# Transposes, copies and differences of an expert's rows in separate steps, and token tables in every second step

## The chip, the core and the metric

The kernel runs on one core of one Trainium2 chip. The time is the device time of one execution in microseconds (us), the median of three runs. A core has a matrix engine (TensorE, PE in the rows, PEld for its weight loads), VectorE (DVE), ScalarE (ACT), GpSimd (POOL) and SyncE (SP), which issues most DMAs. Each engine has its own list of instructions and works through it; semaphores hold an instruction until what it reads is there.

## The reference

Windowed attention, then a mixture of experts, then a gated feed-forward layer. The change lies in the middle part:

```python
def _moe_ref(x, w_gate, w_output_gate, w1, w2):     # x: 2304 x 512, 8 experts, w1: 8 x 512 x 1024, w2: 8 x 1024 x 512
    logits = x @ w_gate
    e_idx = np.argmax(logits, axis=1)
    ...
    for e in range(E):
        mask = e_idx == e
        h = np.maximum(x[mask] @ w1[e], 0.0)
        ye = h @ w2[e]
        out[mask] = gate_w[mask, None] * eom[mask, e, None] * ye
    return out
```

## The kernel before

The attention stage ends with every token's row scattered into the DRAM tensor xs, sorted by expert. The experts are ranked by size; rank p gets room for caps[p] rows: 384, 384, 352, 336, 304, 272, 256, 256. "Expert 3" below is rank 3.

The loop of the expert stage treats experts 0 to 6, each in 16 steps. Steps 0 to 7 are the first layer: step m computes one block of 128 hidden features on TensorE (L1423, tile oh), ScalarE writes its relu hh (L1431), VectorE the remainder hl (L1437). Every number is held as a high part and a low part, which is why each product takes three passes: high rows with high weights, low rows, then low weights. Steps 8 to 15 are the second layer: step kk multiplies block kk of hh and hl into four output tiles oy (L1447). The last expert and the dense layer follow from a table of steps written out by hand, in which the last expert's first layer is L1217.

Behind the matmuls of every step, behind_step does work for later. It takes up to two items of weights that SP has loaded: for an expert's weight ScalarE copies the high part (L461, tile w) and VectorE, or GpSimd for every third, subtracts to get the low part (L463). A 64-bit weight of the dense layer takes two ScalarE operations (L405, L406) and two merges on VectorE (L412, L417). As each item frees its staging tile (there are seven), w_load issues the next load on SP. After that, behind_step draws once from the generator tokens, that is token_order followed by overflow_tables (L890 to L1014). These are small VectorE operations that work out which token each sorted row belongs to, three groups of six comparisons (L941, tile tbl), each followed by six small matmuls on TensorE (L947, tile oid_ps) and a sum (L952, L954), and at the end the tables of overflow blocks, which two DMAs of ScalarE's queue (L1009, L1014) write to DRAM. The generator has 40 pieces, drawn in the steps of experts 0 and 1 and of expert 2's first layer.

In the first four steps of an expert's second layer, emit_xT prepares the rows of the next expert: VectorE transposes a quarter of the features (L1067, tile t, two buffers), ScalarE copies it rounded (L1070, xh), and VectorE forms the difference (L1071, xl). In step 12 (kk = 4) load_x loads the rows of the expert after that into xr, which has one buffer, by four DMAs on SP.

For expert 0 the transposes are made on TensorE instead (L1075 to L1077); that part stays.

The order on every engine in this stage is the order of the code (a manual schedule). The functions that the change touches:

Of the kernel before, what the change touches and what calls it, by code (L numbers as in the profile page):

```python
# [7 lines left out]
F32 = mybir.dt.float32  # L8
# [5 lines left out]
AF = mybir.ActivationFunctionType  # L14
ALU = mybir.AluOpType
# [131 lines left out]
def attn_moe_glu_kernel(ctx, tc, q, k, v, w_gate, w_ogate, w1, w2, w2_gate, w2_val, w2_out, out, caps=CAPS):  # L147
    nc = tc.nc
    B, H, S, D = q.shape
    NT, DM = out.shape  # L150
    E = w_gate.shape[1]
# [8 lines left out]
    KD = DM // 128  # L160
    KF = FF // 128
    KF2 = FF2 // 128
    cap = max(caps)
    CB = -(-cap // 128)
    CP = CB * 128
# [48 lines left out]
    with ExitStack():  # L214
# [811 lines left out]
        def pair_tile(pool, tag, w):  # L1026
            return [pool.tile([128, w], F32R, tag=tag + x, name=tag + x) for x in "hl"]

        def grid(t, n, w):
            return t[:, 0:n * w].rearrange("p (k c) -> p k c", k=n)  # L1030
# [23 lines left out]
        def emit_xT(p, kks=range(KD)):  # L1054
            if p >= E:
                return
            n = caps[p]
            cb = -(-n // 128)
            r = xr[p]
            if p not in xe:  # L1060
                xe[p] = [grid(t, KD, n) for t in pair_tile(xe_p, "x", KD * cap)]
            xh, xl = xe[p]
            for kk in kks:
                if p:
                    nb = -(-n // 32)
                    t = s_p.tile([128, CP], F32, tag="sc", name="t")
                    nc.vector.transpose(  # L1067
                        out=t[:, 0:nb * 32].rearrange("p (b i) -> p b i", i=32), in_=r.rearrange("p b (i k) -> p k b i", k=KD)[:, kk]
                    )
                    nc.scalar.activation(out=xh[:, kk, :], in_=t[:, 0:n], func=AF.Copy)  # L1070
                    TT(out=xl[:, kk, :], in0=t[:, 0:n], in1=xh[:, kk, :], op=ALU.subtract)  # L1071
                    continue
                t = ps_m.tile([128, CP], F32, tag="m", name="tx")
                for c in range(cb):
                    nc.tensor.transpose(t[:, c * 128:c * 128 + 128], features(r[:, c, 0:DM], kk), ident)  # L1075
                nc.scalar.activation(out=xh[:, kk, :], in_=t[:, 0:n], func=AF.Copy)
                TT(out=xl[:, kk, :], in0=t[:, 0:n], in1=xh[:, kk, :], op=ALU.subtract)  # L1077

        yr, x2 = {}, {}

        xraw = [None, None]

        PASSES = ((0, 0), (0, 1), (1, 0))
        HW = KF * cap
# [19 lines left out]
        def behind_step(i0=0):  # L1104
            for i in range(i0, len(plan[step_no[0]])):
                behind_item(i)
            step_no[0] += 1
            if step_no[0] <= E * STEPS:
                next(tokens, None)

        UW = 2 * WU
# [296 lines left out]
        with tc.manual_schedule(engines=ALL_ORDERED):  # L1408
# [5 lines left out]
            for p in range(E - 1):  # L1414
# [29 lines left out]
                for kk in range(KF):  # L1444
                    for d in range(KD):
                        for i, (a, b) in enumerate(PASSES):
                            nc.tensor.matmul(  # L1447
                                out=o[d][:, 0:n],
                                lhsT=wt["w2", p, 0, kk][:, a, d * 128:d * 128 + 128],
                                rhs=(hh, hl)[b][:, kk, :],  # L1450
                                start=(kk == 0 and i == 0),
                                stop=(kk == KF - 1 and i == 2),
                            )
                    if kk % 2:
                        freed[0] += 1
                    if p + 1 < E:
                        if kk < KD:
                            emit_xT(p + 1, (kk,))
                    if kk == KD:
                        if p + 2 < E:  # L1460
                            load_x(p + 2)
                    behind_step()
# [142 lines left out]
```

## Time and profile before

| | |
|---|---|
| median of 3 runs | 828.47 us (828.15 to 829.36) |
| the profiled execution | 831.0 us, of which the span of the trace is 829.3 us |
| TensorE busy in the span | 786.4 us (95%) |
| VectorE busy | 669.2 us (81%) |
| ScalarE busy | 505.2 us (61%) |
| GpSimd busy | 165.0 us (20%) |

The profile shows one execution. Busy time is what an engine spent in instructions; a matmul's end is modelled, so that a busy TensorE is not one at its peak. The granted clock (PEclk) is a share of TensorE's full speed. A wait is the idle time of an engine ahead of an instruction, with the instruction whose end released it; several causes are put down to the last.

### The profile page before, as it was taken

The page shows a single profiled execution, that of the slowest core. Times are in us where ns is not written, and L with a number is a line of the kernel's source. Part 1 is how long each engine was busy: PE and PEld are TensorE (multiplying, and loading weights), DVE is VectorE, ACT ScalarE, POOL GpSimd, SP SyncE. Part 2 cuts the span into 40 slices and gives each one's busy share as a digit, 9 for nine tenths or more (in the row PEclk, how much of TensorE's full clock was granted, in tenths as well). Part 3 has the DMA queues.
Part 4 walks back from the last instruction along what each step waited for, and adds up shares of the span by engine and source line. Part 5 has one row for each costly group of instructions (what it writes and reads, how often), then busy time and mean ns, then how long its engine had stood idle before and what let it go on. Part 6 is the DMA issues. An engine that isn't in the chain of part 4 may idle for free.

```text
span 829.3 us, 17503 instructions
## 1 busy us (share of the span) xinstructions
PE 786.4 (95%) x6031; PEld 727.7 (88%) x6031; DVE 669.2 (81%) x1771; ACT 505.2 (61%) x1355; POOL 165.0 (20%) x249
## 2 busy tenths in 40 slices
PE   8999998979998998798999999999999999999995
PEld 6887784979998998797999999999999999999994
DVE  7899786685887886878999999999877799777642
ACT  6999871445546675666876766765555465554432
POOL 5477775031112122221000000030000003000003
PEclk9999999999998999989999999999999999999998
DMA  9999924867586796797125221131311103111112
GB/s 186 242 222 313 283 92 141 262 204 232 163 250 199 244 281 204 248 279 245 64 65 177 102 102 64 52 115 65 126 51 52 52 26 128 51 52 51 28 50 79
DMA packets 120815, 121.16 MB, mean 146 GB/s; under 512 B 63634, under 2 KB 79634, under 8 KB 120722
## 3 DMA queue, kind: packets, MB, share of 16 engines
q1 hardware_dynamic: 113184, 106.31, 43.6%
q0 software_dynamic: 2880, 9.48, 3.0%
q10 hardware_dynamic: 4658, 4.20, 1.5%
q8 instruction: 49, 0.80, 0.4%
q14 instruction: 44, 0.36, 0.2%
HBM read 89.23 MB, written 30.73 MB: 145 GB/s over the span
## 4 chain that ended last, share of the span: by engine, by line
PE 34%; issue 33%; DVE 11%; DMA 9%; ACT 8%; POOL 2%; SPq 1%; ACTq 0%; DVEq 0%; POOLq 0%
PE pa L1297 6%; PE oo L1320 6%; PE pb L1297 5%; PE oh L1423 4%; DMA rawd<-in_moe_w_gate_dram 3%; PE o L615 3%; ACT w L461 2%; PE s L524 2%; DVE t L1067 2%; POOL out_dram L1335 2%; DVE w L463 2%; PE oh L1217 2%; PE tp L592 1%; DVE rawd L412 1%; DMA raw<-in_moe_w_dram 1%
## 5 line engine op out<-in xcount | busy, mean ns | idle before, releaser
L1320 PE MATMUL oo<-xh,hw 128*128 128x512 f32 x432 | 133.3, 390 | 0.0
L1297 PE MATMUL pa<-w 128*128 128x384 f32 x630 | 127.9, 338 | 0.8 <-ACT wtmp L1158 0.6
L1297 PEld LDWEIGHTS pa<-w 128*128 128x128 f32 x630 | 112.2, 188 | 9.4 <-ACT wtmp L1158 1.3
L1447 PE MATMUL oy<-hh,w 128*128 128x384 f32 (+5 forms) x448 | 103.1, 316 | 0.4 <-DVE hl L1437 0.4
L1335 POOL DMA_INDIRECT out_dram<-ob,oid x18 | 20.5, 1137 | 417.0 <-ACT ob L1158 292.0
L1297 PE MATMUL pb<-w 128*128 128x384 f32 x468 | 94.5, 336 | 0.0
L1423 PE MATMUL oh<-xh,w 128*128 128x384 f32 (+5 forms) x448 | 82.6, 323 | 10.9 <-ACT xh L1070 9.2
L463 POOL TENSOR_TENSOR w<-raw,w 128x512 fp32r<-128x512 f32 x37 | 49.5, 1339 | 193.3 <-ACT w L461 134.9
L1320 PEld LDWEIGHTS oo<-xh,hw 128*128 128x128 f32 x432 | 79.6, 187 | 6.4
L1158 ACT ACTIVATE w<-w 128x256 fp32r<-128x256 f32 (+2 forms) x168 | 76.2, 462 | 14.3 <-DVE w L1185 10.4
L1320 PE MATMUL oo<-xl,hw 128*128 128x512 f32 x216 | 84.4, 391 | 0.0
L1423 PEld LDWEIGHTS oh<-xh,w 128*128 128x128 f32 x448 | 72.9, 197 | 12.6 <-ACT xh L1070 10.5
L1297 PEld LDWEIGHTS pb<-w 128*128 128x128 f32 x468 | 82.7, 188 | 0.4 <-DVE wtmp L1373 0.3
L1447 PEld LDWEIGHTS oy<-hh,w 128*128 128x128 f32 x448 | 77.1, 190 | 1.0 <-DVE hl L1437 0.9
L1158 ACT ACTIVATE wtmp<-pa 128x384 f32<-128x384 f32 x72 | 35.5, 493 | 65.1 <-PE pa L1297 64.8
L461 ACT ACTIVATE w<-raw 128x512 fp32r<-128x512 f32 x112 | 67.7, 623 | 6.3 <-ACT y L1092 5.0
L1447 PE MATMUL oy<-hl,w 128*128 128x384 f32 (+5 forms) x224 | 70.5, 315 | 0.0
L1158 ACT ACTIVATE w<-wraw 128x256 fp32r<-128x256 f32 x108 | 44.6, 415 | 41.4 <-PE pa L1297 25.6
L1373 DVE TENSOR_TENSOR wtmp<-pb,wtmp 128x384 f32<-128x384 f32 x72 | 40.1, 557 | 32.4 <-ACT wtmp L1158 26.3
L1370 DVE TENSOR_TENSOR wtmp<-wtmp 128x384 f32<-128x384 f32 x108 | 58.6, 555 | 6.1 <-ACT wtmp L1376 5.5
L463 DVE TENSOR_TENSOR w<-raw,w 128x512 fp32r<-128x512 f32 x75 | 57.2, 773 | 5.8 <-ACT w L461 4.6
L578 ACT ACTIVATE p<-p,mn 128x128 f32<-128x128 f32 x144 | 56.4, 408 | 0.4 <-DVE mn L557 0.3
(259 smaller groups left out, 1679.9 us busy)
## 6 DMA issues: line engine op xcount, KB each, us to landing
raw<-in_moe_w_dram SPq DMA_DIRECT2D x128, 256.0 KB, 4.3
xs<-zrow SPq DMA_DIRECT2D x8, 774.0 KB, 7.4
rawd<-in_moe_w_gate_dram SPq DMA_DIRECT2D x24, 256.0 KB, 5.0
rawd<-in_moe_w_val_dram SPq DMA_DIRECT2D x24, 256.0 KB, 2.9
rawd<-in_moe_w_out_dram SPq DMA_DIRECT2D x24, 256.0 KB, 3.4
xh<-wo_s SPq DMA_DIRECT2D x24, 256.0 KB, 2.6
xl<-wo_s SPq DMA_DIRECT2D x24, 256.0 KB, 2.9
w<-ys SPq DMA_DIRECT2D x6, 768.0 KB, 6.3
```

The costliest lines, as they stand in the source:

```text
L461: nc.scalar.activation(out=s[:, 0, :], in_=t, func=AF.Copy)
L463: (nc.gpsimd if n_rows[0] % 3 == 0 else nc.vector).tensor_tensor(out=s[:, 1, :], in0=t, in1=s[:, 0, :], op=ALU.subtract)
L578: last_exp[0] = nc.scalar.activation(out=pr[:, c, :], in_=pr[:, c, :], func=AF.Exp, bias=mn[:, c:c + 1], scale=-1.0, accum_out=sums[j][:, ...
L615: nc.tensor.matmul(out=o[64 * a:64 * a + 64, 2 * hf + pp, :], lhsT=raw["vr", j - 1 + i][:, 4 * hf + 2 * pp + a, :], rhs=pm[:, i, 2 * pp + ...
L1158: nc.scalar.activation(out=out, in_=in_, func=AF.Copy)
L1297: nc.tensor.matmul(out=bank_of(j), lhsT=w[:, a, k, :], rhs=x_at(j, b, k), start=(n == 0 and j in (0, 1, 5)), stop=(n == 5), skip_group_che ...
L1320: nc.tensor.matmul(out=o_w[c], lhsT=h_at(s, t)[b][:, b0 * 128:b0 * 128 + 128], rhs=wo_at(s, a), start=(kk == 0 and i == 0), stop=(kk == KF ...
L1335: r = nc.gpsimd.indirect_dma_start(out=out[:, :], out_offset=bass.IndirectOffsetOnAxis(ap=oid[:, 2 * WB * pr + c, :], axis=0), in_=ob, in_ ...
L1370: TT(out=out, in0=a, in1=b, op=ALU.mult)
L1373: TT(out=temp(i), in0=bank_of(j), in1=temp(k), op=ALU.add)
L1423: nc.tensor.matmul(out=o[:, 0:n], lhsT=wt["w1", p, m // 4, kk][:, a, (m % 4) * 128:(m % 4) * 128 + 128], rhs=(xh, xl)[b][:, kk, :], start= ...
L1447: nc.tensor.matmul(out=o[d][:, 0:n], lhsT=wt["w2", p, 0, kk][:, a, d * 128:d * 128 + 128], rhs=(hh, hl)[b][:, kk, :], start=(kk == 0 and i ...
```

## The change

emit_xT keeps only the part for expert 0. A new function turn_step(p + 1, kk), called in every step of the second layer, issues at step i the difference of quarter i - 2, then the transpose of quarter i, then the copy of quarter i - 1. So a quarter's three operations stand in three successive steps, and the group ends in step 5 of the second layer (kk = 5) instead of step 3. And behind_step draws from the generator in every second step: 40 pieces in 80 steps instead of 40.

```diff
             for kk in kks:
-                if p:
...
-                    nc.vector.transpose(
-                        out=t[:, 0:nb * 32].rearrange("p (b i) -> p b i", i=32), in_=r.rearrange("p b (i k) -> p k b i", k=KD)[:, kk]
-                    )
-                    nc.scalar.activation(out=xh[:, kk, :], in_=t[:, 0:n], func=AF.Copy)
-                    TT(out=xl[:, kk, :], in0=t[:, 0:n], in1=xh[:, kk, :], op=ALU.subtract)
-                    continue
...
+        x_turned = []
+
+        def turn_step(p, i):
+
+            if p >= E:
+                return
+            n = caps[p]
+            nb = -(-n // 32)
+            if p not in xe:
+                xe[p] = pair_tile(xe_p, "x", KD * cap)
+            h, low = xe[p]
+            if 0 <= i - 2 < KD:
+                c0 = (i - 2) * n
+                TT(out=low[:, c0:c0 + n], in0=x_turned.pop(0)[:, 0:n], in1=h[:, c0:c0 + n], op=ALU.subtract)
+            if i < KD:
+                t = s_p.tile([128, CP], F32, tag="sc", name="t")
+                nc.vector.transpose(
+                    out=t[:, 0:nb * 32].rearrange("p (b i) -> p b i", i=32),
+                    in_=xr[p].rearrange("p b (i k) -> p k b i", k=KD)[:, i],
+                )
+                x_turned.append(t)
+            if 0 <= i - 1 < KD:
+                c0 = (i - 1) * n
+                nc.scalar.activation(out=h[:, c0:c0 + n], in_=x_turned[-2 if i < KD else -1][:, 0:n], func=AF.Copy)
+            if i == KD + 1:
+                xe[p] = [grid(t, KD, n) for t in xe[p]]
...
             step_no[0] += 1
-            if step_no[0] <= E * STEPS:
+            if step_no[0] % 2 == 0:
                 next(tokens, None)
...
-                    if p + 1 < E:
-                        if kk < KD:
-                            emit_xT(p + 1, (kk,))
+                    turn_step(p + 1, kk)
```

Three places show how the order of instructions moves. The first is VectorE in the second layer of expert 5, where the rows of expert 6 are prepared (t the transposed quarter, xl the difference, w, rawd and wraw the weight work behind each step). Before:

```order
L1067 STREAM_TRANSPOSE t<-xr 128x256
L1071 TENSOR_TENSOR xl<-t,xh 128x256
L463 TENSOR_TENSOR w<-raw,w 128x512
L412 SCALAR_TENSOR_TENSOR rawd<-rawd 128x256
L417 SCALAR_TENSOR_TENSOR wraw<-rawd 128x2x128
L1067 STREAM_TRANSPOSE t<-xr 128x256
L1071 TENSOR_TENSOR xl<-t,xh 128x256
L463 TENSOR_TENSOR w<-raw,w 128x512
L1067 STREAM_TRANSPOSE t<-xr 128x256
L1071 TENSOR_TENSOR xl<-t,xh 128x256
```

and now (the new lines are L1090 for the transpose and L1087 for the difference):

```order
L1090 STREAM_TRANSPOSE t<-xr 128x256
L463 TENSOR_TENSOR w<-raw,w 128x512
L1087 TENSOR_TENSOR xl<-t,xh 128x256
L1090 STREAM_TRANSPOSE t<-xr 128x256
L412 SCALAR_TENSOR_TENSOR rawd<-rawd 128x256
L417 SCALAR_TENSOR_TENSOR wraw<-rawd 128x2x128
L1087 TENSOR_TENSOR xl<-t,xh 128x256
L1090 STREAM_TRANSPOSE t<-xr 128x256
L463 TENSOR_TENSOR w<-raw,w 128x512
L1087 TENSOR_TENSOR xl<-t,xh 128x256
L463 TENSOR_TENSOR w<-raw,w 128x512
L412 SCALAR_TENSOR_TENSOR rawd<-rawd 128x256
```

The difference stood right behind its transpose; now weight work and the next transpose stand between, and the last differences come behind the weight work of two more steps.

The second is VectorE in the second layer of expert 0, where the tables stand between the transposes of expert 1's rows. Before:

```order
L941 TENSOR_SCALAR tbl<-iota_82,far 128x128 x2
L1067 STREAM_TRANSPOSE t<-xr 128x384
L1071 TENSOR_TENSOR xl<-t,xh 128x384
L941 TENSOR_SCALAR tbl<-iota_82,far 128x128 x2
L463 TENSOR_TENSOR w<-raw,w 128x512 x2
L941 TENSOR_SCALAR tbl<-iota_82,far 128x128 x2
L463 TENSOR_TENSOR w<-raw,w 128x512 x2
```

and now, at the end of expert 1's first layer and the start of its second, where these comparisons have gone:

```order
L1455 SCALAR_TENSOR_TENSOR hl<-oh,hh 128x384
L463 TENSOR_TENSOR w<-raw,w 128x512
L941 TENSOR_SCALAR tbl<-iota_82,far 128x128 x2
L1090 STREAM_TRANSPOSE t<-xr 128x352
L412 SCALAR_TENSOR_TENSOR rawd<-rawd 128x256
L417 SCALAR_TENSOR_TENSOR wraw<-rawd 128x2x128
L1090 STREAM_TRANSPOSE t<-xr 128x352
L463 TENSOR_TENSOR w<-raw,w 128x512
L941 TENSOR_SCALAR tbl<-iota_82,far 128x128 x2
```

The comparisons of the first group left expert 0's second layer, and with them the six matmuls that read them.

The third is ScalarE around the two overflow DMAs. Before, in the last two steps of expert 2's first layer (hh the relu, xh the copy of expert 3's rows):

```order
L406 ACTIVATE rawd<-rawd 128x256
L1009 DMA ov_pad<-oi 128x17
L1431 ACTIVATE hh<-oh 128x352
L461 ACTIVATE w<-raw 128x512
L1014 DMA ov_er<-er 1x34
L1070 ACTIVATE xh<-t 128x336
```

and now, in the last steps of expert 4's second layer (y the copy of its results, hh the relu of expert 5):

```order
L461 ACTIVATE w<-raw 128x512
L1009 DMA ov_pad<-oi 128x17
L461 ACTIVATE w<-raw 128x512
L405 ACTIVATE rawd<-rawd 128x256
L406 ACTIVATE rawd<-rawd 128x256
L461 ACTIVATE w<-raw 128x512
L1014 DMA ov_er<-er 1x34
L1110 ACTIVATE y<-oy 128x304
```

Both DMAs moved by 39 and 40 steps, to the end of expert 4. SP's load of the block count moved likewise, from the first layer of expert 2 to that of expert 4.

## Rows read from the trace of the kernel before

**Rows 1.** Busy time by stretch (us), the expert stage; instructions in brackets.

```profile
core 0: us, PE busy (x) PEld busy (x) DVE busy (x) ACT busy (x) POOL busy (x), PEclk, DMA share, GB/s
147.00:382.00 235.00, 214.11 (x1376) 210.19 (x1375) 178.79 (x370) 135.08 (x316) 48.36 (x38) 0.95 0.75 234
```

**Rows 2.** Waits: who waited for whom; us in total, times, longest.

```profile
ACT xh L1070 <- DVE t L1067: 48.6, 28, 2.8
...
DVE xl L1071 <- ACT xh L1070: 14.9, 28, 0.7
...
DVE rawd L412 <- ACT rawd L406: 12.2, 14, 2.0
...
PE oh L1423 <- ACT xh L1070: 9.2, 4, 3.5
...
PE oid_ps L947 <- DVE tbl L941: 5.8, 4, 3.3
...
ACT hh L1431 <- DVE oi L1008: 5.6, 1, 5.6
```

**Rows 3.** TensorE in order of time, and its clock behind the gaps.

```profile
185.29 0.37 PE L947 MATMUL oid_ps<-tbl 128*128 128x36 bf16 x2 [3.25 <-DVE tbl L941]
...
259.10 0.65 PE L1423 MATMUL oh<-xh,w 128*128 128x336 f32 x1 [3.46 <-ACT xh L1070]
...
320.45 0.40 PE L1423 MATMUL oh<-xh,w 128*128 128x272 f32 x1 [2.29 <-ACT xh L1070]
...
185.30:189.50 4.20, 4.20 (x15) 4.14 (x16) 1.40 (x4) 0.98 (x2) 0.00 (x0) 0.51 1.07 218
259.00:264.00 5.00, 4.90 (x17) 4.90 (x18) 4.71 (x8) 4.49 (x12) 1.45 (x1) 0.50 0.74 199
320.00:327.00 7.00, 6.55 (x52) 6.55 (x53) 5.90 (x9) 5.82 (x14) 2.88 (x2) 1.00 0.63 182
```

**Rows 4.** Starts of the second layers of experts 1 to 3, and two first transposes.

```profile
206.37 0.34 PE L1447 MATMUL oy<-hh,w 128*128 128x384 f32 x1
...
239.11 0.32 PE L1447 MATMUL oy<-hh,w 128*128 128x352 f32 x1
...
276.02 0.32 PE L1447 MATMUL oy<-hh,w 128*128 128x336 f32 x1
...
208.81 0.80 DVE L1067 STREAM_TRANSPOSE t<-xr 128x352 f32<-128x352 f32 x1
...
279.94 0.75 DVE L1067 STREAM_TRANSPOSE t<-xr 128x320 f32<-128x320 f32 x1
```

**Rows 5.** VectorE in order of time: the rows of expert 3 prepared.

```profile
247.94 0.80 DVE L1067 STREAM_TRANSPOSE t<-xr 128x352 f32<-128x352 f32 x1
249.30 0.51 DVE L1071 TENSOR_TENSOR xl<-t,xh 128x336 fp32r<-128x336 f32 x1 [0.55 <-ACT xh L1070]
249.82 0.69 DVE L463 TENSOR_TENSOR w<-raw,w 128x512 fp32r<-128x512 f32 x1
250.54 0.43 DVE L412 SCALAR_TENSOR_TENSOR rawd<-rawd 128x256 int32<-128x256 int32 x1
...
259.08 0.51 DVE L1071 TENSOR_TENSOR xl<-t,xh 128x336 fp32r<-128x336 f32 x1 [0.55 <-ACT xh L1070]
```

**Rows 6.** Busy time from one expert's first transpose to the next one's.

```profile
208.80:247.90 39.10, 38.91 (x239) 38.37 (x239) 31.95 (x81) 20.59 (x48) 6.73 (x6) 1.00 0.67 201
...
279.90:310.00 30.10, 30.10 (x210) 30.10 (x210) 24.19 (x44) 19.96 (x48) 6.75 (x5) 1.00 0.81 246
310.00:341.00 31.00, 26.76 (x202) 25.95 (x201) 23.44 (x44) 19.55 (x48) 7.04 (x6) 1.00 0.74 238
341.00:371.70 30.70, 27.21 (x205) 26.81 (x204) 22.49 (x44) 19.46 (x48) 7.63 (x6) 0.89 0.80 250
```

**Rows 7.** VectorE in order of time: one of the last table operations.

```profile
246.23 0.17 DVE L1008 CAST oi<-row 128x17 int32<-128x17 f32 x1
```

**Rows 8.** The page's costliest groups: low parts of weights, on GpSimd and VectorE.

```profile
L463 POOL TENSOR_TENSOR w<-raw,w 128x512 fp32r<-128x512 f32 x37 | 49.5, 1339 | 193.3 <-ACT w L461 134.9
...
L463 DVE TENSOR_TENSOR w<-raw,w 128x512 fp32r<-128x512 f32 x75 | 57.2, 773 | 5.8 <-ACT w L461 4.6
```

More of the change, by code (lines that the diff above doesn't have):

```diff
@@ L1063, in emit_xT @@
             for kk in kks:
-                if p:
-                    nb = -(-n // 32)
-                    t = s_p.tile([128, CP], F32, tag="sc", name="t")
-                    nc.vector.transpose(
-                        out=t[:, 0:nb * 32].rearrange("p (b i) -> p b i", i=32), in_=r.rearrange("p b (i k) -> p k b i", k=KD)[:, kk]
-                    )
-                    nc.scalar.activation(out=xh[:, kk, :], in_=t[:, 0:n], func=AF.Copy)
-                    TT(out=xl[:, kk, :], in0=t[:, 0:n], in1=xh[:, kk, :], op=ALU.subtract)
-                    continue
                 t = ps_m.tile([128, CP], F32, tag="m", name="tx")
```

## The prediction, written before the changed kernel ran

> **What bounds the kernel now.** I read the profile in this order: busy time by stage, who waits for whom in the expert stage, the idle rows of TensorE in order of time, then VectorE and ScalarE around the points where TensorE stands still. The change touches only the expert stage, 147 to 382 us. TensorE is busy there for 214.1 of 235 us, and its mean granted clock is 0.95 [rows 1]; so 20.9 us are idle, and some more is lost at half speed. The reader is to see that TensorE's idle time lies at two kinds of place. One is the matmuls of the token tables: 5.8 us in four waits by the view of waits, nearly all inside the second layer of expert 0; the longest, 3.25 us, is shown [rows 2, 3]. The other is the head of an expert, where the first matmuls wait for the copied input rows xh: 9.2 us at four heads [rows 2]; 3.46 us at expert 3 and 2.29 us at expert 5 are shown [rows 3].
>
> The clock falls with the long gaps. [...] So the first two gaps cost a further 4.2 x 0.49 = 2.1 us and 5.0 x 0.50 = 2.5 us.
>
> Behind the heads stands VectorE. It starts the transposes for expert 2 at 208.81, 2.4 us after TensorE began the second layer (206.37); those for expert 3 at 247.94, 8.8 us after 239.11; those for expert 4 at 279.94, 3.9 us after 276.02 [rows 4, 5]. What made it 6.4 us later in the cycle before expert 3 is table work: from one first transpose to the next VectorE is busy 31.95 us there, and 24.19 us in a cycle without tables [rows 6], 7.8 us less. In a group of transposes each step also holds a round trip: ScalarE waits for the transpose (48.6 us in 28 waits), then VectorE waits for ScalarE's copy (14.9 us in 28 waits, 0.53 each) before it may form the difference [rows 2, 5].
>
> **The change, part by part.**
>
> *Tables half as dense: the table matmuls of expert 0.* The generator is called 40 times; before in steps 0 to 39 (experts 0, 1 and the first layer of 2), now in every second step to step 79, the end of expert 4. The comparisons that feed the first group of table matmuls stood two steps ahead of them, now four, and the group moves from the second layer of expert 0 to that of expert 1. VectorE's lag at that layer was 2.4 us, and a step of TensorE is some 2.0 us (239.11 - 206.37 = 32.7 us for sixteen), so the results are there when TensorE asks [rows 4]. The matmuls themselves stay. Gain: 5.8 + 2.1 = 7.9 us. Bounds: 5, if half the wait turns up at the head of expert 1, to 8.
>
> *Head of expert 3.* The calls in the cycle before it are now eight instead of sixteen, and the light ones. VectorE's busy time there falls from 31.95 by some 7 us, and its four waits of 0.53 go. That is under 25 us for the same 32.7 us of TensorE, so its lag falls from 8.8 to the least that the rows show, 2.4 us. From the first transpose (247.94) the last copied rows took until 259.05 (the last difference starts at 259.08, once the copy is there): 11.1 us [rows 5]. Even unchanged, 2.4 + 11.1 = 13.5 us is earlier than TensorE's question, which came at 259.10 - 3.46 = 255.6, 16.5 us after that layer began. Gain: 3.46 + 2.5 = 6.0 us. Bounds 2 (a short gap and the clock dip stay) to 6.
>
> *What the spacing does to a head by itself.* It takes from VectorE's path four waits of 0.55 us, and about one of 0.7 us in which the merge of a 64-bit weight waited for a ScalarE that the copy had held up (that group waits 12.2 us in 14 times [rows 2]). But the last difference now stands two steps after the last transpose: behind it are the weight work of steps 3 and 4, about 2.2 us (two subtractions of 0.69 and a pair of merges of 0.43). From first transpose to last difference: 11.6 - 2.2 - 0.7 + 2.2 = 10.9 us, and TensorE needs the differences four matmuls later than the copies, 0.7 us (32.7 us for 192 matmuls). So a head is free after some 10.2 us instead of 11.1: I take 0.7 us as the gain of one head. Moving the differences back thus takes most of what the spacing gives here; what is left comes from the engine's whole cycle.
>
> *Experts 4 to 6, where VectorE and ScalarE set the pace.* The three cycles of 30.1, 31.0 and 30.7 us have 24.19, 23.44 and 22.49 us of VectorE work, and 5.9, 7.6 and 8.2 us idle [rows 6]. From each idle time I take 4 x 0.53 + 0.6 = 2.7 us. ScalarE can supply this: it is busy 20 us per cycle [rows 6] and now waits for VectorE, not VectorE for it. To the first I add the table calls 29 to 36, to the second 37 to 40. Of the 7.8 us, the last four calls hold seven short operations of 0.17 us [rows 7], 1.1 us; the calls 25 to 28 hold four short ones, 0.7; so 6.0 us fall into the first cycle. That gives 24.2 + 6.0 + 3.2 = 33.4 (+3.3), 23.4 + 1.1 + 4.9 = 29.4 (-1.6) and 22.5 + 5.5 = 28.0 (-2.7): together -1.0 us. The first cycle begins with a lag of 2.4 instead of 3.9 us, -1.5, and the last head gives -0.7. Gain: 3.2 us. Bounds: a loss of 5, if the idle time does not shrink, to a gain of 13.
>
> *Edits at nothing.* The two overflow DMAs, on ScalarE's queue, move from the first layer of expert 2 to the second of expert 4. There ScalarE stood 5.6 us for the first of them [rows 2]; queued behind it are weight copies, then the y copies and the relu of expert 5. I cost that at nothing more, because ScalarE stood at a copy there anyway; without that cover it is up to 5.6 us, inside the bound. SP's register load of the block count moves from expert 2 to expert 4, behind weight loads that wait for the same VectorE steps; POOL's index iota moves likewise, and POOL is busy for 48 of the stage's 235 us [rows 1]. The load of the next rows stays in its step and comes as much earlier as the last transpose. The number of DMAs is the same.
>
> *POOL against VectorE.* The VectorE subtraction of a weight row takes 0.69 us alone [rows 5] and 0.773 on average over 75; POOL makes 37 of 1.339 us [rows 8]. That is 75 x 0.083 = 6 us in all, 0.17 per POOL operation, and I add nothing, as some VectorE operation was in its way before too. [...]
>
> **Sum.** 7.9 + 6.0 + 3.2 = 17.1 us. The profiled execution took 831.0 us, 1.7 more than its span of 829.3 and 2.5 more than the median of the runs, 828.47. Its time would become 813.9; I take the same off the median: 811.4 us.
>
> **Rivals.**
> 1. *All waits at heads go.* With the round trips gone ScalarE no longer works in bursts, the weight loads come earlier, and TensorE alone sets the pace. For it: VectorE's work (22.5 to 24.2 us) is under TensorE's 27 us busy in the late cycles. Against it: VectorE's 178.8 us [rows 1] would then fill 87% of the stage. Gain: 20.9 us idle, and of the clock's 0.05 x 235 = 12 us what does not lie in idle time, about 10: some 30 us, 798 us.
> 2. *The wait only changes its place.* The copy stands on ScalarE behind the weight work of the step before; if ScalarE is the late one, VectorE waits for it two steps on, the last difference comes 2 us later, and the tables are paid in experts 4 and 5. Then the spacing does not do what it says. Against it: ScalarE waits 48.6 us for transposes. Gain 7.9 + 6.0 - 5 = 8.9 us: 820 us.
> 3. *Slower: tables where VectorE is already the bound.* In experts 4 and 5 each microsecond of VectorE moves a head one for one. If the 7.8 us come whole, ScalarE's 5.6 us for the overflow DMA pass through, and the differences come 2 us later at three heads, that is 19.4 us against 13.9 gained early: 834 us. It decides once the late experts lose more than 13.9 us; against it, no wait at a head is over 3.5 us now [rows 2], and VectorE has 5.9 + 7.6 us idle to absorb tables.
>
> **How the numbers follow.** My forecast 0.57 (804 to 818), rival 1 0.13, rival 2 0.20, rival 3 0.07, something else 0.03. A difference of 0.2%, 1.7 us, is about what a measurement can tell from none. Faster: all of the first two, most of rival 2: 0.88; within 0.2%: 0.03; slower: 0.09. The range of 801 to 822 leaves out rival 3 and the ends of rival 1.
>
> **What would show it.** Right: no idle of TensorE over 1 us at the table matmuls, now in expert 1; no gap at the head of expert 3, and no half clock after it; the waits of the difference for the copy near zero, those of the copy for the transpose well under 48.6 us; heads of experts 5, 6 and 7 that wait for xl, not xh. Wrong: the waits of 14.9 us turn up again under the difference or the merges; gaps over 4 us at experts 5 to 7; a long wait of ScalarE at the overflow DMA with a late relu behind it. A first transpose in expert 3's second layer more than 4 us after that layer's start would show the third part mis-sized.

## The result, and the profile after

The changed kernel takes 810.2 us (median of 4 runs, 807.86 to 810.96); the kernel before, on the same chip, 828.91 us. The ratio is 0.9759, 95% interval 0.972 to 0.9798, so 17 to 23 us are gained; 17.1 were forecast. In a second comparison the same file gave 0.9746 (0.9714 to 0.9779).

In all rows behind the change the transposes are L1090, the difference L1087, the copy L1097, the matmuls oh L1441 (last expert L1235) and oy L1465, the relu L1449 and hl L1455. The profiled execution took 809.85 us, its span is 808.1.

Busy time by stretch, from the first matmul of expert 0 to the head of the last expert (145.0 to 359.7 us), answers to [rows 1]; the same stretch before, 147.3 to 380.6, had 212.41 us of TensorE in 233.3:

```profile
145.00:359.70 214.70, 208.07 (x1373) 206.11 (x1371) 180.36 (x373) 137.97 (x323) 49.98 (x38) 0.98 0.85 260
```

TensorE's idle time fell from 20.9 to 6.6 us, the clock rose from 0.96 to 0.98, and VectorE's busy time did not fall (177.42 before). What went is waiting. The view of waits for 140 to 365 us answers to [rows 2]:

```profile
ACT xh L1097 <- DVE t L1090: 30.0, 24, 3.3
...
DVE rawd L412 <- ACT rawd L406: 8.2, 11, 1.8
...
PE oh L1441 <- DVE xl L1087: 4.3, 2, 2.7
...
ACT y L1110 <- DVE er L1013: 2.4, 1, 2.4
...
PE oh L1235 <- DVE xl L1087: 1.8, 1, 1.8
```

A wait of the difference for the copy (14.9 us before) no longer appears; nor does a wait of a table matmul. TensorE in order of time, all its waits over 1 us in the stage behind the first transposes, and its clock behind two of them, answer to [rows 3]:

```profile
303.00 0.40 PE L1441 MATMUL oh<-xl,w 128*128 128x272 f32 x1 [1.66 <-DVE xl L1087]
...
332.43 0.58 PE L1441 MATMUL oh<-xl,w 128*128 128x256 f32 x1 [2.66 <-DVE xl L1087]
...
359.69 0.39 PE L1235 MATMUL oh<-xl,w 128*128 128x256 f32 x1 [1.79 <-DVE xl L1087]
...
303.00:308.00 5.00, 5.00 (x27) 5.00 (x28) 2.82 (x7) 1.80 (x4) 1.28 (x1) 0.66 0.77 216
332.40:337.00 4.60, 4.57 (x21) 4.57 (x22) 2.46 (x6) 2.21 (x7) 0.66 (x1) 0.50 1.05 291
```

Heads 1 to 4 have no gap; those of experts 5, 6 and 7 wait for xl. Second layers of experts 1 to 3 and the first transposes in them, answering to [rows 4]:

```profile
195.56 0.34 PE L1465 MATMUL oy<-hh,w 128*128 128x384 f32 x1
...
227.82 0.32 PE L1465 MATMUL oy<-hh,w 128*128 128x352 f32 x1
...
258.51 0.32 PE L1465 MATMUL oy<-hh,w 128*128 128x336 f32 x1
...
198.98 0.79 DVE L1090 STREAM_TRANSPOSE t<-xr 128x352 f32<-128x352 f32 x1
...
229.88 0.81 DVE L1090 STREAM_TRANSPOSE t<-xr 128x352 f32<-128x352 f32 x1
...
261.22 0.73 DVE L1090 STREAM_TRANSPOSE t<-xr 128x320 f32<-128x320 f32 x1
```

VectorE's lag is 3.4, 2.1 and 2.7 us, where it was 2.4, 8.8 and 3.9. Busy time from one first transpose to the next, answering to [rows 6]:

```profile
198.90:229.80 30.90, 30.90 (x193) 30.74 (x192) 26.38 (x52) 20.50 (x48) 5.99 (x5) 1.00 0.79 240
...
261.20:292.40 31.20, 31.20 (x217) 31.20 (x216) 29.87 (x70) 20.38 (x48) 8.27 (x7) 1.00 0.85 251
292.40:321.40 29.00, 27.34 (x198) 27.02 (x197) 23.18 (x52) 18.79 (x46) 5.64 (x5) 0.94 0.78 239
321.40:349.30 27.90, 24.71 (x181) 24.27 (x181) 23.18 (x44) 19.73 (x51) 7.54 (x6) 0.88 0.90 275
```

Where the time came from is read from the times at which TensorE passed the same points of the stage. The points are the start of expert 0's second layer, the start of expert 1, the start of expert 3's second layer ([rows 4] and above) and the last gap at the head of the last expert. Before, and then now (the last point now, 359.69, stands above):

```profile
164.52 0.34 PE L1447 MATMUL oy<-hh,w 128*128 128x384 f32 x1
...
189.47 0.86 PE L1423 MATMUL oh<-xh,w 128*128 128x384 f32 x4
...
380.57 0.58 PE L1217 MATMUL oh<-xh,w 128*128 128x256 f32 x1 [2.76 <-ACT xh L1070]
...
162.28 0.34 PE L1465 MATMUL oy<-hh,w 128*128 128x384 f32 x1
...
178.92 0.86 PE L1441 MATMUL oh<-xh,w 128*128 128x384 f32 x4
```

| kernel (profiled execution) | expert 0's second layer | to expert 3's second layer | to the last expert | gained against before, in this order |
|---|---|---|---|---|
| before | 24.95 | 86.55 | 104.55 | |
| the change | 16.64 | 79.59 | 101.18 | 8.3 + 7.0 + 3.4 |
| e1_tables | 16.64 | 83.39 | 111.87 | 8.3 + 3.2 - 7.3 |
| e2_spacing | 18.54 | 79.38 | 96.37 | 6.4 + 7.2 + 8.2 |

The change gains 18.6 us up to the last expert. Behind that point it gains 2.0 more in the last expert's first layer (12.58 us before, 10.59 now), where the clock was 0.77 for 7.4 us before and is 1.00 for 6.3 us now. A further 2.2 us of the difference in span lie ahead of the stage, which began at 147.26 before and 145.03 now, and 1.7 are lost from the last expert's second layer to the end. Nothing was changed in either place, and the start of the stage differs as much between other executions (145.00 us in e2b_spacing, 147.25 in e6_one_earlier), so neither is counted as the change's.

### The profile page after: what moved, and what is told of

Read it like the earlier page. It is cut to its first block, busy times and chain, and to the rows that moved or that the text cites. A ratio compares the mean times of both kernels' runs of the same rounds, so it can differ in the third digit from the quotient of the medians.

```text
span 808.1 us, 17509 instructions
## 1 busy us (share of the span) xinstructions
PE 780.0 (97%) x6031; PEld 724.3 (90%) x6031; DVE 669.7 (83%) x1771; ACT 504.9 (62%) x1355; POOL 164.9 (20%) x249
## 4 chain that ended last, share of the span: by engine, by line
PE 50%; issue 33%; DVE 8%; DMA 2%; ACT 2%; POOL 2%; SPq 0%; ACTq 0%; another core or an unknown queue 0%; DVEq 0%; POOLq 0%
PE oh L1441 11%; PE oy L1465 9%; PE pa L1315 7%; PE oo L1338 6%; PE pb L1315 5%; PE o L615 3%; PE s L524 3%; POOL out_dram L1353 2%; PE tp L592 2%; PE tq L498 1%; PE oy L1256 1%; PE oh L1235 1%; DVE p L557 1%; DVE xtok L686 1%; DVE w L463 1%
## 5 line engine op out<-in xcount | busy, mean ns | idle before, releaser
L1465 PE MATMUL oy<-hh,w 128*128 128x384 f32 (+5 forms) x448 | 101.1, 312 | 0.0
L1441 PE MATMUL oh<-xh,w 128*128 128x384 f32 (+5 forms) x448 | 81.0, 321 | 0.5 <-ACT xh L1097 0.5
L1465 PEld LDWEIGHTS oy<-hh,w 128*128 128x128 f32 x448 | 75.8, 188 | 0.0
L1441 PEld LDWEIGHTS oh<-xh,w 128*128 128x128 f32 x448 | 72.2, 197 | 1.2 <-ACT xh L1097 0.7
L1465 PE MATMUL oy<-hl,w 128*128 128x384 f32 (+5 forms) x224 | 69.8, 312 | 0.0
L463 DVE TENSOR_TENSOR w<-raw,w 128x512 fp32r<-128x512 f32 x75 | 52.4, 706 | 5.2 <-ACT w L461 4.9
```

Source lines behind the costliest of these rows:

```text
L463: (nc.gpsimd if n_rows[0] % 3 == 0 else nc.vector).tensor_tensor(out=s[:, 1, :], in0=t, in1=s[:, 0, :], op=ALU.subtract)
L1441: nc.tensor.matmul(out=o[:, 0:n], lhsT=wt["w1", p, m // 4, kk][:, a, (m % 4) * 128:(m % 4) * 128 + 128], rhs=(xh, xl)[b][:, kk, :], start= ...
L1465: nc.tensor.matmul(out=o[d][:, 0:n], lhsT=wt["w2", p, 0, kk][:, a, d * 128:d * 128 + 128], rhs=(hh, hl)[b][:, kk, :], start=(kk == 0 and i ...
```

## The experiments

Ratios are to the kernel before, run beside each kernel on the same chip (829.7 to 830.3 us there). "Apart" means in a different step. The last column adds three rows of the view of waits; VectorE's wait for the relu (hl for hh, 16.7 us before and 18.0 in e0) is not in it.

| kernel | copy apart from transpose | difference apart from copy | tables drawn | time, us | ratio (95%) | VectorE waited for ScalarE: xl + w + rawd, us |
|---|---|---|---|---|---|---|
| before | no | no | every step to 39 | 828.47 | 1 | 14.9 + 4.6 + 12.2 = 31.7 |
| e1_tables | no | no | every second | 824.55 | 0.9939 (0.9918 to 0.9961) | 14.8 + 3.2 + 16.1 = 34.1 |
| e3_copy_same | no | yes | every second | 832.58 | 1.0045 (1.0026 to 1.0063) | 1.5 + 22.9 + 20.2 = 44.6 |
| e8_diff_same | yes | no | every second | 805.16 | 0.9716 (0.9677 to 0.9755) | 0.2 + 2.0 + 7.9 = 10.1 |
| e0_both (the change) | yes | yes | every second | 808.67 | 0.9746 (0.9714 to 0.9779) | 0 + 3.9 + 7.7 = 11.6 |
| e2b_spacing | yes | yes | every step to 39 | 805.37 | 0.9696 (0.9674 to 0.9718) | 0 + 6.4 + 6.4 = 12.8 |
| e7_no_tables | yes | yes | never | 803.09 | 0.9686 (0.9648 to 0.9724) | 0 + 6.1 + 7.4 = 13.5 |

**e0_both** is the changed kernel unedited, as the measure for its companions.

> The changed kernel itself, timed again beside the parts of it on one chip. Every theory expects about 810 us, a ratio of 0.976 to the kernel before.

**e1_tables**, the tables alone:

```diff
-            if step_no[0] <= E * STEPS:
+            if step_no[0] % 2 == 0:
                 next(tokens, None)
```

> Only the tables in every second step; transpose, copy and difference as before. Theory 1 (tables make the early waits, round trips the late ones): the waits at the table matmuls and at the head of expert 3 go (7.9 + 6.0 us), but experts 4 and 5 get 6.0 + 1.1 us of table work on a VectorE that still has its round trips, less 1.5 us of lag: 13.9 - 5.6 = 8.3 us faster, 820.5 us, with gaps at the heads of experts 5 to 7 as large as before or larger. Rival (the tables do all of it, the spacing only moves the last difference back): 18 us faster, 810 us. Rival (the spacing does all of it): no change, 829 us.

It gains 5 us, where 8.3 were expected. TensorE in order of time shows the table waits gone, but gaps over 1.5 us come in the heads and steps behind, two of which stand here. The third line is the start of expert 2's second layer, the fourth the first transpose of expert 3's rows on VectorE:

```profile
245.89 0.42 PE L1423 MATMUL oh<-xh,w 128*128 128x336 f32 x1 [1.52 <-ACT xh L1070]
...
310.89 0.59 PE L1423 MATMUL oh<-xh,w 128*128 128x272 f32 x1 [2.73 <-ACT xh L1070]
...
226.87 0.32 PE L1447 MATMUL oy<-hh,w 128*128 128x352 f32 x1
...
234.75 0.79 DVE L1067 STREAM_TRANSPOSE t<-xr 128x352 f32<-128x352 f32 x1
```

The table wait of expert 0 is worth 8.3 us here by itself, by the same points of time as above. Up to expert 3's second layer thinner tables gain only 3.2 us, and the late experts give 7.3 back. VectorE's lag before expert 3's rows is still 7.9 us (8.8 before).

**e2_spacing**, the separated steps alone, and **e2b_spacing**, the same again with more rounds:

```diff
-            if step_no[0] % 2 == 0:
+            if step_no[0] <= E * STEPS:
                 next(tokens, None)
```

> Only the spacing; tables in every step as before, ending in expert 2. Theory 1: VectorE reaches the comparisons of expert 0 about 2.9 us earlier, so of the 5.8 us at the table matmuls about half stays (gain 5 with the clock); the lag at expert 3 falls from 8.8 to some 6 us, which nearly closes its gap (gain 5); experts 4 to 6 carry no tables and lose 2.7 us of idle in each cycle (gain 8): 18 us faster, 811 us, about as fast as both edits together, by other waits: a wait of some 3 us at the table matmuls is to be seen, none over 1.5 us at experts 5 to 7. Rival (the tables do all of it): 829 us, or slower by the later differences. Rival (the spacing does all of it): 809 us, and then the tables alone change nothing.

> The spacing alone once more, as the kernel that the next three stand beside on the same chip: 806.7 us as in its first run, a ratio of 0.972 to the kernel before.

The first gave 806.66 us, 0.9716 (0.9685 to 0.9747); the second is in the table. So the separated steps alone carry the whole gain, and the tables could have stayed dense. Two waits of TensorE in the first of these runs:

```profile
178.00 0.35 PE L947 MATMUL oid_ps<-tbl 128*128 128x36 bf16 x2 [1.35 <-DVE tbl L941]
...
329.63 0.39 PE L1441 MATMUL oh<-xl,w 128*128 128x256 f32 x1 [2.67 <-DVE xl L1087]
```

Of 5.8 us in table waits 1.35 are left although the tables are as dense as before, and head 3 has no gap. By stretches the gain is 6.4, 7.2 and 8.2 us. The expectation had the size nearly right (811 us) and two of its signs wrong: it wanted some 3 us of table wait and no gap over 1.5 us at experts 5 to 7, where 2.67 and 2.46 us stand at experts 6 and 7.

**e3_copy_same** puts the copy back into the step of its transpose; the difference comes a step later. **e8_diff_same** is its counterpart: the copy stays a step behind the transpose, and the difference comes in the copy's step. Both keep the thin tables.

The edit of e3_copy_same:

```diff
-            if 0 <= i - 2 < KD:
-                c0 = (i - 2) * n
+            if 0 <= i - 1 < KD:
+                c0 = (i - 1) * n
...
-            if 0 <= i - 1 < KD:
-                c0 = (i - 1) * n
-                nc.scalar.activation(out=h[:, c0:c0 + n], in_=x_turned[-2 if i < KD else -1][:, 0:n], func=AF.Copy)
+            if i < KD:
+                c0 = i * n
+                nc.scalar.activation(out=h[:, c0:c0 + n], in_=t[:, 0:n], func=AF.Copy)
...
```

> Tables in every second step as in the changed kernel; the copy in the same step as its transpose, the difference one step later. It keeps the gap between copy and difference, but VectorE's next operation, the weight subtraction, now waits until ScalarE has made both the copy and the weight's high part, up to 1.0 us per step. Theory 1 (the round trip is what costs): more than half of the spacing's gain is lost, 812 to 817 us, with some 20 us of waits of the weight subtraction or the merges for ScalarE. Rival (the last difference's place binds; it is a step earlier here): 805 to 807 us, faster than the changed kernel.

And that of e8_diff_same:

```diff
-            if 0 <= i - 2 < KD:
-                c0 = (i - 2) * n
-                TT(out=low[:, c0:c0 + n], in0=x_turned.pop(0)[:, 0:n], in1=h[:, c0:c0 + n], op=ALU.subtract)
...
                 nc.scalar.activation(out=h[:, c0:c0 + n], in_=x_turned[-2 if i < KD else -1][:, 0:n], func=AF.Copy)
+                TT(out=low[:, c0:c0 + n], in0=x_turned.pop(0)[:, 0:n], in1=h[:, c0:c0 + n], op=ALU.subtract)
...
```

> The changed kernel with one separation taken back: the copy still stands a step behind its transpose, but the difference stands in the same step as the copy (behind the next transpose), so that VectorE may wait for ScalarE again. Theory 3, formed from the run with copy and transpose in one step: what carries the gain is that ScalarE never stands at a transpose with weight copies queued behind it; the difference's own step matters little. It expects 805 to 812 us, waits of the copy for the transpose near 30 us, waits of the weight subtraction for ScalarE's copy as in the changed kernel, and under 8 us of waits of the difference for the copy. The rival, the reason of the prediction (the 14.9 us in which VectorE waited for the copy are what the cycle gets back): those waits return at 0.3 to 0.6 us each, a cycle is 2 to 3 us longer, and the time is 818 to 824 us.

With e1 and e0 these make a square of four. By the medians, moving only the difference costs 8 us against e1, moving only the copy gains 19, and moving both gains 16. e3 missed both ranges of its expectation: the waits of the weight work were 43 us instead of some 20, and it ended slower than the kernel before. The rival of e8's expectation falls: hardly any wait of the difference came back. The rows show why. ScalarE (start, length) and then VectorE in e3_copy_same, at the first quarters of expert 5's rows:

```profile
306.18 0.43 ACT L1097 ACTIVATE xh<-t 128x272 fp32r<-128x272 f32 x1 [4.69 <-DVE t L1090]
306.52 0.61 ACT L461 ACTIVATE w<-raw 128x512 fp32r<-128x512 f32 x1
307.04 0.42 ACT L405 ACTIVATE rawd<-rawd 128x256 f32<-128x256 f32 x1
307.36 0.42 ACT L406 ACTIVATE rawd<-rawd 128x256 int32<-128x256 uint32 x1
310.28 0.43 ACT L1097 ACTIVATE xh<-t 128x272 fp32r<-128x272 f32 x1 [2.51 <-DVE t L1090]
...
305.47 0.68 DVE L1090 STREAM_TRANSPOSE t<-xr 128x288 f32<-128x288 f32 x1
307.81 1.03 DVE L412 SCALAR_TENSOR_TENSOR rawd<-rawd 128x256 int32<-128x256 int32 x1 [1.66 <-ACT rawd L406]
308.87 0.42 DVE L417 SCALAR_TENSOR_TENSOR wraw<-rawd 128x256 int32<-128x256 int32 x1
309.22 0.43 DVE L1087 TENSOR_TENSOR xl<-t,xh 128x272 fp32r<-128x272 f32 x1
309.57 0.68 DVE L1090 STREAM_TRANSPOSE t<-xr 128x288 f32<-128x288 f32 x1
```

ScalarE stands at the copy until the transpose is done (4.69 us), and the step's weight copies are queued behind that copy. VectorE, done with the transpose, then needs those weight results and stands 1.66 us. The two engines take turns. The difference is no longer in the way, but it had filled part of that wait before: against e1, 13.3 us of its own waits went and 23.8 us of waits of the weight work came. The same quarters in e8_diff_same, ScalarE and then VectorE:

```profile
292.95 0.43 ACT L1094 ACTIVATE xh<-t 128x272 fp32r<-128x272 f32 x1 [3.45 <-DVE t L1087]
293.29 0.62 ACT L461 ACTIVATE w<-raw 128x512 fp32r<-128x512 f32 x1
294.32 0.43 ACT L1094 ACTIVATE xh<-t 128x272 fp32r<-128x272 f32 x1 [0.42 <-DVE t L1087]
...
292.24 0.68 DVE L1087 STREAM_TRANSPOSE t<-xr 128x288 f32<-128x288 f32 x1
292.85 0.38 DVE L412 SCALAR_TENSOR_TENSOR rawd<-rawd 128x256 int32<-128x256 int32 x1
293.26 0.42 DVE L417 SCALAR_TENSOR_TENSOR wraw<-rawd 128x256 int32<-128x256 int32 x1
293.61 0.68 DVE L1087 STREAM_TRANSPOSE t<-xr 128x288 f32<-128x288 f32 x1
294.21 0.40 DVE L1095 TENSOR_TENSOR xl<-t,xh 128x272 fp32r<-128x272 f32 x1
294.53 0.69 DVE L463 TENSOR_TENSOR w<-raw,w 128x512 fp32r<-128x512 f32 x1
```

ScalarE still stands at the first copy for 3.45 us, but the weight work of the transpose's step now stands ahead of that copy in its queue, and was done before the wait began. VectorE goes from the transpose into the merges without a wait, and the difference in the copy's own step finds its copy ready. The reason for the gain is thus the place of the copy in ScalarE's queue against the weight copies, not the wait of the difference. e3 and the change bear this out from the other side: on VectorE both have, in each step, a difference, a transpose and then weight work, and what moves between them is the copy on ScalarE (and, by one step, which quarter the difference treats). Not run was the copy behind the weight copies of its own transpose's step, which would move the place in the queue alone.

**e4_tables_early** draws in expert 0's first layer, not in its second, in every step of expert 1 and in every second step from expert 2 on, beside the separated steps:

```diff
-            if step_no[0] % 2 == 0:
+            if step_no[0] <= KF or 2 * KF < step_no[0] <= 4 * KF or step_no[0] > 4 * KF and step_no[0] % 2 == 0:
```

> With the spacing; the generator is drawn in the first layer of expert 0, in every step of expert 1 and in every second step of experts 2 and 3, so that the tables end before expert 4 and none stand in the second layer of expert 0. Theory 1: keeps the early gains (7.9 + 6.0) and takes some 7 us of VectorE work out of the two cycles of experts 4 and 5: 3 to 5 us faster than both edits together, 805 to 807 us, with the gaps at experts 5 and 6 under 1 us. Rival (the late heads are bound by loads or by ScalarE, not by VectorE's work): within 1 us of both edits together, 810 us, with the same gaps. Rival (the tables need to be thin everywhere): 812 us or more, with a new gap at the head of expert 2 or 3.

It gave 807.24 us, 0.972 (0.9693 to 0.9747): no better than e2, and its 1.4 us against the change are within the intervals. A gap of 1.73 us stands at expert 5, where under 1 us was expected. By stretches it gains 8.3, 6.9 and 7.0 us, so taking table work out of experts 4 and 5 does pay there. But behind its gap of 2.46 us at the last expert the clock was 0.50 for 3.6 us, and that expert's first layer took 13.0 us instead of 10.6.

**e7_no_tables** is the changed kernel without token tables (the order of tokens is left out, so result rows land in wrong places):

```diff
-            tokens = token_order()
+            nc.vector.memset(nov, 0.0)
+            nc.vector.tensor_copy(oid[:, :, 0], tokid)
+            tokens = iter(())
```

> The changed kernel without the token tables and overflow tables altogether (the order of tokens is left out, so that result rows land in wrong places; the DMAs that read the tables stay). It bounds what any placement of the tables can be worth. Theory 2, that table work beside the separated steps hides in VectorE's idle time in the experts where TensorE is the bound: 802 to 806 us, the time of the kernel with tables in steps 0 to 39 (805 to 807 us) or just below it. The rival, that the tables in every second step cost experts 3 and 4 what VectorE spends on them: 7.8 us of work and the waits at heads 5 and 6 fall away, 797 to 801 us.

The 803.09 us lies in the range of theory 2, and can't be told from e2b_spacing's 805.37: beside separated steps the dense tables cost 2 us in the medians, within the intervals. To the change itself (0.9746 and 0.9759) the gap is 5 to 6 us of 830, and the intervals overlap by a little. That thin tables cost more than dense ones is likely, not settled.

**e5_last_ahead** is e2 with the last difference a step earlier, in step 4 ahead of that step's merges; **e6_one_earlier** is e2 with the whole group a step earlier, beginning in the last step of the first layer:

The edit of e5_last_ahead:

```diff
-                    turn_step(p + 1, kk)
+                    if kk != KD + 1:
+                        turn_step(p + 1, kk)
...
-                    behind_step()
+                        behind_item(0)
+                        turn_step(p + 1, KD + 1)
+                        behind_step(1)
+                    else:
+                        behind_step()
```

> The spacing alone (tables in every step), with the last difference pulled ahead of the two merges of step 4. Theory 2a (the place of the last difference makes the waits left at the heads of experts 6 and 7): each of the waits of 2.7 and 2.5 us for xl falls by 0.9 us, 1.7 us in all, and up to 4 us if the clock then holds: 803 to 805 us. Theory 2b (VectorE's and ScalarE's whole cycle is the bound, and the head is only where it shows): no change, 806.7 us; the waits at the heads shrink and come back as later relus and remainders.

And that of e6_one_earlier:

```diff
+                    if m == KF - 1:
+                        turn_step(p + 1, 0)
...
-                    turn_step(p + 1, kk)
+                    turn_step(p + 1, kk + 1)
```

> The spacing alone, with the whole group one step earlier: the first transpose in the last step of the first layer, the last difference in step 4 of the second. Theory 2a: the last difference comes one step, some 1.3 to 1.8 us, earlier at each head, so the waits for xl at experts 6 and 7 fall to about 1 us and the clock holds: 802 to 804 us. Theory 2b: 806 to 807 us, as VectorE does the same work per cycle.

e5 gave 805.34 us, 0.969 (0.9668 to 0.9712), the time of e2b. The waits for xl at heads 6 and 7 went, and smaller waits for hl (0.54 and 1.37 us) and xh (1.15 us) came instead. The equal time does not show that the last difference's place is worth nothing (theory 2b). In the profiled execution the stretch from expert 3's second layer to the last expert took 92.7 us, against 96.4 in e2 and 96.1 in e2b, so 3.4 to 3.7 us were gained there, as theory 2a had it. But expert 0's second layer took 21.9 us instead of 18.5. There the difference now stands ahead of comparisons; TensorE waited 1.80 and 1.03 us for them instead of 1.35, and its clock was 0.55 for 5.2 us. The edit without expert 0 was not run. e6 gave 811.22 us, 0.9768 (0.9745 to 0.979), about 6 us slower than e2b. One place of it is plain in the view of TensorE in order of time: expert 0's second layer, where transposes now stand ahead of the comparisons, waits 2.52 us at a table matmul:

```profile
181.87 0.35 PE L947 MATMUL oid_ps<-tbl 128*128 128x36 bf16 x2 [2.52 <-DVE tbl L941]
```

That layer takes 21.3 us (164.51 to 185.80) instead of 18.5 in e2. Of the rest, in the profiled executions, 2.2 us against e2b lie ahead of the stage (it begins at 147.25 instead of 145.00), where the edit changes nothing, and the stretch from expert 3's second layer to that of the last expert is 0.5 us longer. Whether the edit has a part in the first is not shown.

## Why the prediction was right, and where its reasons were not

**The sum.** 17.1 us forecast, 18.6 measured up to the last expert in the profiled executions, by terms 7.9, 6.0 and 3.2 against 8.3, 7.0 and 3.4. The sizes were right. Of the reasons, the first credit is shared by both edits, the second was given mainly to the wrong edit, and the third came out by luck, from two errors of opposite sign.

**Tables half as dense, expert 0 (7.9).** 8.3 measured. The wait is gone, and so is the clock of 0.51 for 4.2 us behind it, from which the 2.1 us were worked out ([rows 3]): now it is 1.00 from 162.3 to 195.5 us. e1 shows that thinner tables do this alone. But e2 shows that separated steps alone do nearly the same (6.4), so the two edits share this gain instead of adding up. The prediction did not price that overlap.

**Head of expert 3 (6.0).** 7.0 measured up to that expert's second layer, 6.2 of it behind the start of expert 2's (36.91 us before, 30.69 now, [rows 4]), and no gap is left, nor the clock of 0.50 for 5.0 us that gave the 2.5 us ([rows 3]): it is 1.00 from 227.8 to 258.5 us. The step that failed is the one that makes table work the cause: "VectorE's busy time there falls from 31.95 by some 7 us". With thinner tables alone it fell to 27.84 us in a cycle of 35.78; the lag stayed at 7.9 us, and the gain was 3.2. With separated steps alone VectorE kept 30.17 us of work in a cycle of 32.68; the lag fell to 3.9 us, and the gain was 7.2. The lag was made of VectorE's work plus its waits for ScalarE, and the waits decided.

**The spacing at a head by itself (0.7).** It was forecast as a gain (the working gives 11.1 - 10.2 = 0.9) and is a loss. From the first transpose to the end of TensorE's wait the heads of experts 5, 6 and 7 took 10.4, 10.2 and 8.8 us before and take 10.6, 11.0 and 10.3 now. As forecast they wait for xl: the last differences now stand behind two more steps of weight work, and that took more than the waits saved. At expert 7 VectorE waited 0.74 us for ScalarE in these steps (357.52 us), and at expert 6 the last difference, begun 0.18 us behind a POOL subtraction, took 1.50 us instead of 0.42 (last section). e5 and e8, which have the last difference a step earlier, show no wait for xl at these heads.

**Experts 4 to 6 (3.2 in all with the last head).** 3.4 measured. The three cycles, forecast at 33.4, 29.4 and 28.0 us, came as 31.2, 29.1 and 27.9, so they gained 3.7 us instead of 1.0. The shorter lag gave 1.2 instead of 1.5, and the last head lost 1.5 instead of gaining 0.7: that the total fits is luck. The mis-sized term is the 2.7 us taken "from each idle time": VectorE's idle time fell by 4.6, 1.8 and 3.5 us ([rows 6] and above). In the first of these cycles VectorE is busy 29.87 of 31.20 us, so only 1.3 us are idle, where 3.2 had been left. The price of the round trip was read mainly off the wait of the difference (14.9 us), which was the wrong row to act on. In e0 that wait went whole and the merges' wait for ScalarE fell from 12.2 to 7.7; e3, which took away nearly all of the 14.9 alone, became slower than the kernel before. Whether "moving the differences back" costs time beside a copy that stands apart is not settled: e8 is 3.5 us faster than e0 in the medians, but their intervals overlap.

**Edits at nothing.** Right for the change: ScalarE stands 2.0 and 2.4 us around the two overflow DMAs (5.6 for the first before). A wait of 2.82 us of VectorE for the relu stands behind the second (310.47 us), and TensorE does not wait there. In e8, where expert 5 has no gap for xl, TensorE does wait there: 1.79 us for the y copy behind that DMA (307.93 us).

**POOL against VectorE.** The page's costliest groups answer to [rows 8], and the third row is the difference in the view by line (687 ns mean, 495 before):

```profile
L463 POOL TENSOR_TENSOR w<-raw,w 128x512 fp32r<-128x512 f32 x37 | 49.9, 1348 | 170.2 <-ACT w L461 117.5
...
L463 DVE TENSOR_TENSOR w<-raw,w 128x512 fp32r<-128x512 f32 x75 | 52.4, 706 | 5.2 <-ACT w L461 4.9
...
L1087 DVE TENSOR_TENSOR xl<-t,xh 128x256 fp32r<-128x256 f32 (+5 forms) x28 | 19.2, 687 | 0.0
```

The 28 differences became 5.4 us longer, the 75 weight subtractions 4.8 us shorter. Five differences, each begun 0.10 to 0.20 us behind a POOL subtraction, took 1.50 to 1.65 us, and none took over 0.73 before, when weight subtractions begun 0.35 to 0.43 us behind one took 1.42 to 1.79 us. So the long operations are partly others now, and the sum is nearly the same, as forecast. But one of the five is the last difference of expert 6, on which TensorE waits (last section).

**The rivals.** All waits at heads going (rival 1) did not happen in the change, but dense tables come within 7.4 to 8.7 us of its 798. A wait that only changes its place (rival 2) is refuted for the change and shown for e3, where the difference's wait reappears at w and rawd. Rival 3 is refuted for this change: the late experts gained. Its mechanism is real in e1, which gives 7.3 us back there.

**A version that beats the change.** Dense tables with separated steps (0.9696, e5 0.969), or only the copy a step later (0.9716), are 3 to 5 us faster in the medians; some of the intervals overlap with the change's.

## What to carry to other kernels

When two engines pass a small result to and fro, look at what is queued behind the waiting instruction: here the harm was not VectorE's wait for ScalarE's copy, but that ScalarE, standing at that copy, kept back weight results that VectorE needed next (43.1 us of waits for them in e3_copy_same, 11.6 in the change). Moving the one instruction that stands and waits behind the independent work of its queue was enough here, and moving its consumer too bought nothing that the runs could show. Price such an edit by all waits between the two engines in the stage together, and try two edits alone before crediting each with its part, since both can remove the same wait. When a variant takes the same time, compare it stretch by stretch: in e5 a gain and a loss of nearly the same size stand behind it.

## What the runs showed of the hardware

In these runs the length of a gap alone did not tell whether TensorE's clock fell behind it. In the changed kernel, after 2.66 us of waiting (332.43 us, above) the granted clock was 0.50 for 4.6 us and after 1.66 us it was 0.66 on average over 5.0 us; in e2_spacing after 2.67 us it stayed at 1.00 for 5.0 us, after 2.46 us it was 0.59 over 3.9 us:

```profile
329.60:334.60 5.00, 4.97 (x42) 4.97 (x43) 2.89 (x6) 2.33 (x7) 1.06 (x1) 1.00 1.05 270
356.10:360.00 3.90, 3.89 (x20) 3.89 (x21) 1.74 (x4) 0.57 (x3) 0.00 (x0) 0.59 1.02 369
```

In the changed kernel the five VectorE differences that began 0.10 to 0.20 us behind a POOL subtraction took 1.50 to 1.65 us, the others of the same experts' rows 0.42 to 0.55. The last two differences of expert 6's rows on VectorE, and POOL:

```profile
328.91 0.42 DVE L1087 TENSOR_TENSOR xl<-t,xh 128x256 fp32r<-128x256 f32 x1
...
330.87 1.50 DVE L1087 TENSOR_TENSOR xl<-t,xh 128x256 fp32r<-128x256 f32 x1
...
330.69 1.41 POOL L463 TENSOR_TENSOR w<-raw,w 128x512 fp32r<-128x512 f32 x1 [4.02 <-ACT w L461]
```

The second difference begins 0.18 us behind POOL's subtraction and lasts 1.1 us longer than its equal one step earlier. Over all operations the sums nearly cancel (5.4 us more and 4.8 us less, above), but here it counts: the difference ends at 332.37 us and TensorE's wait of 2.66 us at 332.43, so some 1.1 us of that wait (an estimate, 1.50 less 0.42) come from the longer difference.
